# v of one chunk moves from SyncE's queue to a casting DMA on GpSimd's queue

## The chip, the cores and the metric

The kernel runs on one core of a Trainium2 chip. Its metric is the device time of one execution in microseconds (us), the median over several executions. A profile is one further execution, recorded by the hardware profiler; its times are counted from the first instruction of the program.

## What is computed

Two layers in sequence. The first is a retention layer over q, k, v of shape (4 batches, 8 heads, 768 positions, 64):

```
state = gamma[h] * state + outer(k[t], v[t])        # one 64x64 state per batch and head
y[t]  = scale * q[t] @ state
```

The second is an MLP on the 3072 x 512 result: `out = gelu_tanh(y @ w_in) @ w_out`, with w_in 512 x 2048 and w_out 2048 x 512. All inputs and the output are float32 in device memory; the kernel's matmuls take float16.

## The kernel before

**Chunks.** The 768 positions are cut into six chunks c = 0..5 of 128 positions. Inside a chunk, retention becomes matmuls for each of the four batches b: a score matrix a = k q^T (`mm_A`, L273) masked by the decay (`ev_A` on VectorE, L286), y from the old state (`mm_yc`, L295) plus y from the scores and v (`mm_yi`, L308), and the new state from k and v (`mm_s`, L327; evicted by `ev_S`, L344; decayed on GpSimd by `decay`, L353). y, transposed, is the xT of the MLP: `moe1` (L434) with a gelu on ScalarE (L449), then `moe2` (L479), evicted by L501 or L499 and written out by L506.

**Preparation.** q and k come in twice from chunk 2 on. `load_blk` (L110) brings q and k in 32 x 32 blocks, 16 DMAs of 64 KB for each, so that VectorE's 32 x 32 transpose (`tr`, L263) finishes the transposition without TensorE; `load1` (L98) brings v and the plain k with one DMA of 256 KB for each batch. GpSimd multiplies the decay factors into q, kT and k (`prep_blk` L206, `prep1` L195) and casts v to float16 (L192), each into float16 tiles. `prep(c, "QKvk")` is that order: q blocks, kT blocks, v, plain k.

**What sets the order.** The schedule is written out by hand. Every engine executes its instructions in the order in which the program issues them, and waits at the head when an operand is missing. `run(units, after)` (L520) issues a list of matmul units, and after the unit with a given number the extra steps named in the dictionary. So TensorE works on the MLP of chunk c while the retention of chunk c+1 is slipped in between. The stretch of interest is the two `run` calls of chunk 1: the first (L673) does `moe1` of chunk 1, and after its units 7, 8 and 10 prepares chunk 2; the second (L690) does `moe2` of chunk 1 with the retention of chunk 2 in it: after unit 3 come the scores of batches 0 and 1, after 7 those of batches 2 and 3, after 11 `att_Y`, after 12 to 15 the states. The loop at L705 repeats that for the later chunks.

**Queues.** SyncE's queue (SP) holds nearly all loads, one long sequence: q blocks 2, kT blocks 2, three late stores of chunk 0, v 2 (four DMAs), k 2 (four), then `load(3)` = q blocks 3, kT blocks 3 and v and k of chunk 3 in turn, then chunk 4 and so on. GpSimd's queue (POOL) carries, in one order with GpSimd's arithmetic, the weights at the start (w_in L418, w_out L425: float32 in memory, float16 in SBUF, so these DMAs cast) and most stores of the output (L506). Eight semaphores are taken in turn by SP's DMAs, so that each DMA waits for the landing of the eighth before it.

**Buffers.** The raw v tiles have 6 buffers (`v32`), the float16 v tiles 8 (`v16`, two chunks), the raw kT block has one (`kT32`), the raw q block two.

Of the kernel before, what the change touches and what calls it, by code (L numbers as in the profile page):

```python
# [9 lines left out]
F16 = mybir.dt.float16  # L10
# [6 lines left out]
def kernel(  # L17
# [9 lines left out]
    nc = tc.nc  # L27
    B, H, S, Dh = q.shape
    C = 128
# [27 lines left out]
    pre = ctx.enter_context(tc.tile_pool(name="pre", bufs=2 * B))  # L57
# [31 lines left out]
    def ld_tile(nm, c, b):  # L89
        if nm == "q":  # L90
            t = ld_all(("q32", c)).rearrange("p (b hp) a d -> p b (hp a d)", b=B)
            return t[:, b].rearrange("p (h d) -> p h d", h=H)
        if (nm, c, b) not in raw:
            raw[nm, c, b] = ld.tile([128, H, Dh], F32, tag=f"{nm}32", bufs=6, name=f"{nm}32")
        return raw[nm, c, b]

    def load1(eng, nm, c, b):
        eng.dma_start(  # L98
            out=ld_tile(nm, c, b),
            in_=srcs[nm][b, :, c * C:(c + 1) * C, :].rearrange("h p d -> p h d"),  # L100
        )

    def load_blk(nm, c):
        t = ld_all((nm + ("32" if nm == "q" else "T32"), c))
        src = srcs[nm].rearrange("b (hp j) s (dd d) -> j dd s (b hp) d", j=2, dd=2)
        for j in range(2):
            for dd in range(2):
                for a in range(4):
                    p0, t0 = (2 * j + dd) * 32, c * C + a * 32
                    nc.sync.dma_start(  # L110
                        out=t[p0:p0 + 32, :, a, :], in_=src[j, dd, t0:t0 + 32]
                    )

    def load(c):
        for nm in "qk":
            if c in BLK[nm]:
                load_blk(nm, c)
        for b in range(B):
            for nm in "vk":
                load1(nc.sync, nm, c, b)  # L120
# [22 lines left out]
    for j in range(2):  # L143
# [3 lines left out]
        out=iden,  # L147
        in_=iden,
# [7 lines left out]
        out=mask.rearrange("p j hp t -> p (j hp) t"),  # L156
        in_=mask.rearrange("p j hp t -> p (j hp) t"),
# [7 lines left out]
        out=misc[:, 0:1], in_=zero[:, 0:1], func=AF.Gelu_apprx_tanh, scale=1.0  # L165
# [14 lines left out]
    h16 = {}  # L180
# [345 lines left out]
    VE, AC, PO, SY = nc.vector, nc.scalar, nc.gpsimd, nc.sync  # L526
# [132 lines left out]
    load_blk("k", 2)  # L659
    for rows, o_sb in late:  # L660
        nc.sync.dma_start(out=rows, in_=o_sb)
    for nm in "vk":
        for b in range(B):
            load1(SY, nm, 2, b)
    load(3)

    def prep(c, nms):

        for nm in nms:
# [12 lines left out]
            3: [(att_S, 1, 2)],  # L682
            4: [(att_AY, 1, (3,), "o", 1, (), VE)],
            6: [(att_S, 1, 3)],
            7: [(prep, 2, "Q")],
            8: [(tr, 2, "q")],
            10: [(prep, 2, "Kvk")],
        },
    )
    run(  # L690
# [33 lines left out]
    c = NCk - 1  # L724
# [36 lines left out]
```

## Time and profile before

| | us |
|---|---|
| median of 5 executions (lowest to highest) | 213.19 (211.78 to 215.31) |
| the profiled execution's own time | 213.38 |
| its span, first to last instruction | 211.3 |
| TensorE busy in the span | 204.1 (97%) |
| VectorE, ScalarE, GpSimd busy | 91.6, 83.7, 101.1 |
| granted TensorE clock, mean over the span | 1.000 |

The span is 2.1 us shorter than the profiled execution's own time; what lies around it is taken as fixed. The other views used below are the list of waits (who waited for whom: total, times, longest), the timeline (start and length of a group of instructions, in brackets the idle time before it and what ended it) and sums by window (busy time by engine and the mean share of the 16 DMA engines that was busy; it exceeds 1 where packets overlap).

### The profile page before, as it was taken

Reading aid. Unit: us, or ns where it says so; the run is one execution under the profiler, and the core shown is the slowest. Engines: PE = TensorE matmul, PEld = TensorE weight load, DVE = VectorE, ACT = ScalarE, POOL = GpSimd, SP = SyncE. Lnnn points to the kernel's source line nnn. Section 1 sums busy time; section 2 is a strip of 40 time slices with the busy share of each in tenths; the row PEclk is TensorE's granted clock in tenths of the full one; section 3 lists DMA queues with packets and bytes.
Section 4 is the critical chain, followed back from the end, with each engine's and each line's share of the span. In section 5 each row is a group of like instructions: output and inputs, shape, how many; then the busy total and the mean of one; then the engine's idle time right before and its main releaser. Section 6 shows DMA issues by size and latency. Waiting matters only on the chain.

```text
span 211.3 us, 3863 instructions
## 1 busy us (share of the span) xinstructions
PE 204.1 (97%) x1502; PEld 110.3 (52%) x1502; DVE 91.6 (43%) x163; ACT 83.7 (40%) x142; POOL 101.1 (48%) x123
## 2 busy tenths in 40 slices
PE   7999999999999999999699999999999999999994
PEld 2458444467886465444356444456444446444453
DVE  6787000488543848150856542566560562100001
ACT  2474660345464121664113366113366113466120
POOL 2599300316175749571976949561497711100100
PEclk9999999999999999999999999999999999999999
DMA  7999999997878987968988989888898020100112
GB/s 162 288 236 180 206 201 204 278 251 147 125 112 212 244 179 186 204 107 160 254 160 192 210 151 247 158 168 176 168 232 200 3 101 36 67 0 0 50 50 99
DMA packets 132691, 33.83 MB, mean 160 GB/s; under 512 B 126529, under 2 KB 130881, under 8 KB 132673
## 3 DMA queue, kind: packets, MB, share of 16 engines
q1 hardware_dynamic: 115248, 21.27, 52.1%
q0 software_dynamic: 5696, 8.91, 18.0%
q10 hardware_dynamic: 11728, 3.41, 7.1%
q8 instruction: 11, 0.18, 0.3%
q14 instruction: 8, 0.06, 0.1%
HBM read 31.48 MB, written 6.29 MB: 179 GB/s over the span
## 4 chain that ended last, share of the span: by engine, by line
PE 62%; DMA 19%; SPq 10%; POOL 4%; issue 1%; DVE 1%; POOLq 0%; DVEq 0%
PE o_ps L479 29%; PE h_ps L434 26%; SPq L110 9%; DMA w_out<-in_moe_w_out_dram 8%; DMA k<-in_k_dram 7%; DMA q<-in_q_dram 3%; PE a_ps L273 2%; PE y_ps L308 2%; POOL w_in L418 2%; PE y_ps L295 1%; DMA kT<-in_k_dram 1%; PE s_ps L327 1%; POOL k L195 1%; POOL kT L206 1%; DVE a_sb L286 1%
## 5 line engine op out<-in xcount | busy, mean ns | idle before, releaser
L479 PE MATMUL o_ps<-w_out,g 128*128 128x512 f16 (+1 forms) x400 | 88.6, 371 | 0.0
L434 PE MATMUL h_ps<-xT,w_in 128*128 128x512 f16 (+1 forms) x464 | 85.1, 343 | 0.0
L449 ACT ACTIVATE g<-h_ps 128x512 f16<-128x512 f32 x96 | 56.9, 597 | 47.4 <-PE h_ps L434 47.3
L434 PEld LDWEIGHTS <-w_in 128*128 128x128 f16 x464 | 44.9, 98 | 37.5 <-issue 0.3
L479 PEld LDWEIGHTS <-g 128*128 128x128 f16 x400 | 37.4, 98 | 38.6
L286 DVE TENSOR_TENSOR a_sb<-a_ps,mask 128x512 f16<-128x512 f32 x48 | 30.1, 684 | 16.3 <-PE a_ps L273 16.2
L501 ACT COPY o_sb<-o_ps 128x512 f32<-128x512 f32 x19 | 11.1, 585 | 53.0 <-PE o_ps L479 51.2
L195 POOL TENSOR_TENSOR k<-k,cst 128x512 f16<-128x512 f32 x23 | 24.1, 1066 | 15.3 <-DMA k<-in_k_dram 15.2
L506 POOL DMA_DIRECT2D out_dram<-o_sb x18 | 10.0, 559 | 40.3 <-ACT o_sb L501 33.4
L206 POOL TENSOR_TENSOR kT<-kT,cst 128x512 f16<-128x512 f32 x16 | 16.3, 1047 | 11.0 <-DMA kT<-in_k_dram 10.5
L353 POOL TENSOR_TENSOR stg<-st,cst 128x512 f32<-128x512 f16 x16 | 16.4, 1059 | 6.4 <-DVE st L344 3.9
L263 DVE STREAM_TRANSPOSE qkT<-q 128x512 f16<-128x512 f16 x16 | 11.4, 711 | 15.7 <-POOL q L206 15.7
L206 POOL TENSOR_TENSOR q<-q,cst 128x512 f16<-128x512 f32 x16 | 16.3, 1047 | 2.9 <-DMA kT<-in_k_dram 2.8
L263 DVE STREAM_TRANSPOSE qkT<-kT 128x512 f16<-128x512 f16 x16 | 10.9, 698 | 13.5 <-POOL kT L206 13.5
L344 DVE TENSOR_TENSOR st<-s_ps,stg 64x256 f16<-64x256 f32 x32 | 13.5, 422 | 5.0 <-PE s_ps L327 4.4
L195 DVE TENSOR_TENSOR q<-q,cst 128x512 f16<-128x512 f32 x8 | 5.9, 743 | 17.6 <-DMA q<-in_q_dram 17.6
L192 POOL CAST v<-v 128x512 f16<-128x512 f32 x16 | 9.5, 613 | 7.0 <-DMA v<-in_v_dram 4.1
L226 DVE CAST xT<-y_ps 128x512 f16<-128x512 f32 x11 | 7.2, 687 | 12.9 <-PE y_ps L308 12.9
L517 DVE COPY o_sb<-o_ps 128x256 f32<-128x256 f32 x2 | 0.8, 424 | 26.6 <-PE o_ps L479 26.6
L224 ACT CAST xT<-y_ps 128x512 f16<-128x512 f32 x13 | 7.2, 587 | 11.2 <-PE y_ps L308 11.2
L171 PE MATMUL spin_ps<-zero 128*128 128x512 f16 x30 | 9.2, 443 | 1.3 <-DVE zero L139 1.3
L273 PE MATMUL a_ps<-qkT 64*128 64x128 f16 x192 | 8.3, 218 | 1.9 <-DVE qkT L263 1.6
(39 smaller groups left out, 88.5 us busy)
## 6 DMA issues: line engine op xcount, KB each, us to landing
v<-in_v_dram SPq DMA_DIRECT2D x21, 256.0 KB, 4.3
k<-in_k_dram SPq DMA_DIRECT2D x20, 256.0 KB, 4.3
out_dram<-o_sb POOLq DMA_DIRECT2D x18, 256.0 KB, 3.0
q<-in_q_dram SPq DMA_DIRECT2D x64, 64.0 KB, 2.8
kT<-in_k_dram SPq DMA_DIRECT2D x64, 64.0 KB, 2.8
w_out<-in_moe_w_out_dram POOLq DMA_DIRECT2D x4, 512.0 KB, 15.8
q<-in_q_dram ACTq DMA_DIRECT2D x4, 256.0 KB, 8.6
k<-in_k_dram ACTq DMA_DIRECT2D x4, 256.0 KB, 8.4
```

The source lines that it names most:

```text
L110: nc.sync.dma_start(out=t[p0:p0 + 32, :, a, :], in_=src[j, dd, t0:t0 + 32])
L195: eng.tensor_tensor(out=t, in0=src, in1=cst[:, col:col + H].unsqueeze(2).broadcast_to([128, H, Dh]), op=ALU.mult,)
L206: nc.gpsimd.tensor_tensor(out=t, in0=ld_all((key, c))[:, b * NHP:(b + 1) * NHP].rearrange("p hp a d -> p (hp a) d"), in1=cst[:, col:col + ...
L263: nc.vector.transpose(out=qkT_tile(c, b)[:, "qk".index(nm)].rearrange("p hp t -> p (hp t)"), in_=blk16.pop((nm, c, b)).rearrange("p ha d - ...
L273: nc.tensor.matmul(out=ps[j][:, hp], lhsT=t[j * 64:(j + 1) * 64, 1, hp], rhs=t[j * 64:(j + 1) * 64, 0, hp], start=True, stop=True,)
L286: nc.vector.tensor_tensor(out=s, in0=ps[j], in1=mask[:, j], op=ALU.mult)
L344: eng.tensor_tensor(out=st[sl, :, b, sl], in0=s_ps[sl, :, sl], in1=stg[sl, :, b, sl], op=ALU.add,)
L353: nc.gpsimd.tensor_tensor(out=stg[:, :, b], in0=st[:, :, b], in1=cst[:, OG:OG + NHP].unsqueeze(2).broadcast_to([128, NHP, 128]), op=ALU.mult,)
L434: nc.tensor.matmul(out=out, lhsT=w_in_of(fc, kc), rhs=xT[c][:, kc, t0:t1], start=(kc == 0 and first), stop=(kc == NHP - 1), skip_group_che ...
L449: nc.scalar.activation(out=out, in_=in_, func=AF.Gelu_apprx_tanh, scale=1.0)
L479: nc.tensor.matmul(out=ps[:, n0:n1], lhsT=g_sb[c, fc // 2][:, fc % 2, b * C:(b + 1) * C], rhs=w_out_sb[fc // (NF // NO)][:, fc % (NF // NO ...
L501: nc.scalar.copy(out=o_sb, in_=ps)
```

## The change

v of chunk 2 no longer goes through SP, a float32 tile and a cast on GpSimd. Four DMAs on GpSimd's queue read float32 v and write float16 tiles directly. They stand behind the four q preparations of chunk 2 (after unit 7) and so ahead of the kT preparations (after unit 10). GpSimd's four v casts of chunk 2 are gone. SP goes from the late stores straight to k of chunk 2 and on to `load(3)`. Nothing else differs in order on any engine: TensorE, VectorE and ScalarE have the same instructions in the same sequence. All other chunks load v as before.

```diff
     for rows, o_sb in late:
         nc.sync.dma_start(out=rows, in_=o_sb)
-    for nm in "vk":
-        for b in range(B):
-            load1(SY, nm, 2, b)
-    load(3)
+    for b in range(B):
+        load1(SY, "k", 2, b)
+    load(3)
+
+    def load_v16(c):
+
+        for b in range(B):
+            t = pre.tile([128, H, Dh], F16, tag="v16", bufs=2 * B, name="v16")
+            nc.gpsimd.dma_start(
+                out=t, in_=v[b, :, c * C:(c + 1) * C, :].rearrange("h p d -> p h d")
+            )
+            h16["v", c, b] = t
...
-            7: [(prep, 2, "Q")],
+            7: [(prep, 2, "Q"), (load_v16, 2)],
             8: [(tr, 2, "q")],
-            10: [(prep, 2, "Kvk")],
+            10: [(prep, 2, "Kk")],
```

## The prediction

> **What bounds the kernel now.** I read the page first: TensorE is busy for 204.1 of 211.3 us at a granted clock of 1.000, so only its idle time can be won. The list of waits then says for what it idles inside the run, and TensorE's timeline where.
>
> ```profile
> engine line waited for: us in total, times, longest us
> PE a_ps L273 <- DVE qkT L263: 1.6, 2, 1.0
> PE spin_ps L171 <- DVE zero L139: 1.3, 1, 1.3
> ```
> ```profile
> 97.73 2.75 PE L479 MATMUL o_ps<-w_out,g 128*128 128x512 f16 x12
> 101.47 0.40 PE L273 MATMUL a_ps<-qkT 64*128 64x128 f16 x8 [0.99 <-DVE qkT L263]
> 102.48 0.40 PE L273 MATMUL a_ps<-qkT 64*128 64x128 f16 x8 [0.61 <-DVE qkT L263]
> ```
>
> The spin wait is the start-up; the change does not reach it. The only wait of over 0.5 us after it is 0.99 + 0.61 = 1.60 us at 101.5: the scores of chunk 3 wait for the kT transposes of chunk 3. **So the change can win at most 1.6 us, 0.75%.** The other chunks' scores (69.42, 134.11, 165.96) wait for nothing.
>
> Back from there, in the timelines of GpSimd and of SP:
>
> ```profile
> 60.23 4.07 POOL L206 TENSOR_TENSOR q<-q,cst 128x512 f16<-128x512 f32 x4
> 66.72 4.07 POOL L206 TENSOR_TENSOR kT<-kT,cst 128x512 f16<-128x512 f32 x4 [2.43 <-DMA kT<-in_k_dram]
> ...
> 99.62 4.06 POOL L206 TENSOR_TENSOR kT<-kT,cst 128x512 f16<-128x512 f32 x4 [5.20 <-DMA kT<-in_k_dram]
> ```
> ```profile
> 64.86 1.42 SPq L661 DMA_DIRECT2D out_dram<-o_sb  x3
> 66.37 4.42 SPq L98 DMA_DIRECT2D v<-in_v_dram  x4
> 70.84 3.78 SPq L98 DMA_DIRECT2D k<-in_k_dram  x4
> 74.71 13.13 SPq L110 DMA_DIRECT2D q<-in_q_dram  x16
> 87.95 9.30 SPq L110 DMA_DIRECT2D kT<-in_k_dram  x16
> ```
>
> GpSimd stood idle for 5.20 us before the kT preparation of chunk 3, for a DMA that SP issued at the end of an unbroken queue (64.86 to 97.25). SP's order makes the wait: v, k, q, kT. Every microsecond that SP is earlier arrives at 99.62.
>
> **Gain: the stall at 101.5.** Taking v out removes 4.42 us of issue ahead of k. The gain g in the landing of kT lies between 0.5 and 4.4 us. 4.4 is that whole row. For the low end, DMA engines, not SP, set the pace there; the sums by window are:
>
> ```profile
> 64.00:66.00 2.00, 2.00 (x20) 1.77 (x19) 0.75 (x2) 1.24 (x3) 0.30 (x1) 1.00 0.73 115
> 66.00:72.00 6.00, 6.00 (x43) 2.78 (x41) 3.57 (x6) 1.18 (x2) 4.71 (x6) 1.00 1.08 279
> 72.00:77.00 5.00, 5.00 (x38) 2.34 (x37) 4.03 (x7) 0.58 (x1) 2.94 (x5) 1.00 1.06 240
> 77.00:80.00 3.00, 3.00 (x55) 2.21 (x53) 0.71 (x2) 1.59 (x3) 1.67 (x2) 1.00 0.45 76
> ```
>
> The last two columns are the DMA share and GB/s. From 66 to 77 the engines are full (1.06 to 1.08), and v's bytes are still read in the same stretch. If only the idle shares can be filled, that is 2 x 0.27 = 0.5 us at 64 to 66 (low end) and 3 x 0.55 = 1.7 us more at 77 to 80, where SP issues slowly because the k loads before it have not landed. I take the sum of the bytes: SP alone moves 266 GB/s in such 256 KB loads (the DMA view of 99.5 to 104). Stores of 0.79 MB at 330 GB/s (my estimate, between the 426 and 221 of the slices 67 to 69) take 2.4 us, v and k of 2.1 MB take 7.9 us; from about 65.8 that ends at 76.1, with a microsecond to land 77 against 79.9 before: g = 2.9.
>
> As a row and a rule that speak against the change: the engines' share of 1.06 to 1.08 is the row. The Trainium skill, page "DMA: Bandwidth & Descriptors", section "Rules for kernel authors", says the same of queues in general, that spreading DMAs over SP, ACT and GpSimd gives no bandwidth, since all run on the same 16 engines, and saves only issue time. By that rule alone g would be the 0.5 of the first idle stretch, and the time 212.9; no row decides it.
>
> **Cost: the kT preparation of chunk 2.** The four new DMAs are issued by GpSimd between its q preparations, which end at 60.23 + 4.07 = 64.30, and its kT preparations, which start at 66.72 because their DMA lands then. So 2.4 us of issue are covered by an idle gap. What the trace has for an issue by GpSimd:
>
> ```profile
> L506 POOL DMA_DIRECT2D out_dram<-o_sb x18 | 10.0, 559 | 40.3 <-ACT o_sb L501 33.4 <-DMA kT<-in_k_dram 3.9 <-DVE o_sb L499 3.0
> L418 POOL DMA_DIRECT2D w_in<-in_moe_w_in_dram x6 | 4.6, 782 | 0.0
> L425 POOL DMA_DIRECT2D w_out<-in_moe_w_out_dram x4 | 3.0, 801 | 0.0
> ```
>
> A store takes 0.56. The casting loads are 0.72 to 0.91 each, and 0.73 apart when they follow one another (12.38 to 19.05 for nine, the last at full length). They land in pieces of 1 KB, 256 or 512 for one DMA; the 512 cost hardly more than the 256 (0.74 against 0.71 apart). The new DMAs have 1024 pieces each (128 partitions x 8 heads, 256 B read, 128 B written), which no row shows. Bounds: 0.56 (pieces cost nothing) and 2 x 0.73 = 1.46 (all of the cost is by pieces). By the step from 256 to 512, 1024 pieces come to 0.785; this is the nearest row, and I take it. Four end at 64.30 + 3.14 = 67.44, so the kT preparation is late by d = 0.7.
>
> Who waits: the VectorE transposes of kT for batches 0 and 1 end at 68.51 and 69.52 (rows 67.80 and 68.81, 0.71 each); TensorE's scores start at 69.42, the second eight at 69.75. With 0.06 for the signal the second transpose has 0.17 us in hand. So a stall **s = d - 0.17 = 0.55 us** appears at 69.5 where there was none. Batches 2 and 3 have four microseconds more and hide it. Stores late on SP are not touched: ScalarE reuses the first of their buffers at 69.57, against a landing at 67.3 now.
>
> **The rest.** The four casts of v on GpSimd go (4 x 0.61 = 2.44 us); nothing on the path waited for them: the plain k preparations end at 81.28, TensorE wants the last k at 83.69. They now end earlier, with nothing to gain. v itself: TensorE reads it from 78.54 (batch 0) to 79.3 (batch 3), and the cast v was there at 74.5. Now it is the landing that counts. I put its first packets 1.5 us after the first issue, at 65.8 (an estimate: a store of GpSimd's, of 256 KB too, has landed a median 3.0 us after its issue). The nearest row is SP's 256 B packet, 18 ns on one of 16 engines; the weights' 98 ns for a 1 KB piece is the far end. At 18 to 21 ns, taken by turns with SP's (from 29 to 35 us GpSimd's and ACT's packets are moved 948 to 886), v ends near 76 and has landed by 77.1: two microseconds of cover. If the cover goes, each microsecond of lateness beyond 79.3 + s stalls TensorE one for one.
>
> **Sum.** TensorE's scores of chunk 3 would start at 100.48 if nothing were late; they stand still for 1.6 us. Against that time the end moves to max(s, 1.6 - g). With s = 0.55 and g = 2.9 it is 0.55: the old stall is gone, a third of it comes back in front. Net -1.05 us, 213.38 - 1.05 = **212.3 us** for the profiled execution. This execution is 0.2 above the median of the runs shown (213.19), so against the median it is a gain of 0.4 to 0.5%. 0.5%, 1.07 us, is about what a measurement of this kernel can tell from no change.
>
> **The rivals.**
> - *Issues as cheap as a store's* (0.56 each, d = 0): s = 0, all 1.6 us are won, 211.8. For it: 256 and 512 pieces cost the same. Against: the casting loads' own rows. Chance 0.10.
> - *The main case*, 0.71 to 0.94 each (0.94: the slope from a store's 64 pieces to 512, carried on): net -1.3 to -0.4, 212.0 to 212.9. Chance 0.45, the faster half a little likelier (0.28 to 0.17).
> - *SP gains little* (g under 1.1, DMA engines bound): net max(s, 1.6 - g) - 1.6, with g = 0.5 it is -0.5, 212.9. For it: shares over 1 from 66 to 77. Against: 0.45 at 77 to 80. Chance 0.13.
> - *The issue takes the place of the stall.* Four issues of 1024 pieces hold the kT preparation and with it the scores at 69.5. From 1.05 us an issue, s = 4 x 1.05 - 2.42 - 0.17 = 1.6 and nothing is won; at 1.46, s = 3.25, net +1.65, 215.0: slower. Chance 0.17, half of it above +0.5%.
> - *v lands late* (a small casting packet costs over 30 ns): from there a stall at 78.5 of 1 to several us, at 98 ns some 13. A stall of 1.05 us eats the gain; from 2.1 us on it is slower than before by over 0.5%, 214.5 and more. Chance 0.10.
> - Something unseen on GpSimd's queue, slower: 0.05.
>
> **How the numbers follow.** Faster by over 0.5%: 0.28 + 0.10 = 0.38. Within 0.5%: 0.17 + 0.13 + 0.08 = 0.38. Slower: 0.09 + 0.10 + 0.05 = 0.24. The range goes from 211.5 (all won, less the 0.2 that the profiled execution lies above the median) to 215.0 (the dear issue); beyond it lie most of the late v and the unseen, under 0.2.
>
> **What the new profile would show.** Right: no wait of TensorE's scores at about 101, kT of chunk 3 prepared from about 96.7, a new wait of half a microsecond for qkT near 69.5, four issues near 0.8 us between 64.3 and 67.5, v landed by 77. Wrong: issues of over 1 us; a TensorE wait at 78.5 for a DMA of v; kT of chunk 3 landing after 98.

## The result and the profile after

The changed kernel takes a median of 213.49 us (212.36 to 218.22, 48 executions), the kernel before 212.64 us (211.38 to 215.35, 90 executions). The ratio is 1.004, with a 95% interval of 1.0026 to 1.0054 (intervals stand in brackets below): the change costs some 0.85 us, where 0.4 to 0.5% of gain was forecast. The profiled execution of the changed kernel took 213.94 us, span 211.8 us, at a granted clock of 1.00 in every stage shown. One later profile, that of e9_k_on_pool, fell in an execution of 305.14 us at a granted clock of 0.661 and is not read; all others ran at 0.992 to 1.000.

TensorE's list of waits in the changed kernel (total, times, longest):

```profile
PE a_ps L273 <- DVE qkT L263: 1.9, 2, 1.3
PE spin_ps L171 <- DVE zero L139: 1.3, 1, 1.3
```

Its line for qkT read 1.6, 2, 1.0 before. It looks like the same wait, but TensorE's timeline (changed kernel, the two stretches that matter) shows that it is another:

```profile
65.77 3.62 PE L479 MATMUL o_ps<-w_out,g 128*128 128x512 f16 x16
70.65 0.40 PE L273 MATMUL a_ps<-qkT 64*128 64x128 f16 x8 [1.26 <-DVE qkT L263]
71.67 0.40 PE L273 MATMUL a_ps<-qkT 64*128 64x128 f16 x8 [0.61 <-DVE qkT L263]
...
99.74 2.75 PE L479 MATMUL o_ps<-w_out,g 128*128 128x512 f16 x12
102.43 0.62 PE L273 MATMUL a_ps<-qkT 64*128 64x128 f16 x16
```

The wait at 101 is gone (no bracket at 102.43), and a larger one stands at 69.4 to 71.7: the scores of chunk 2 wait 1.26 + 0.61 = 1.87 us for kT of chunk 2, where nothing waited before. GpSimd's timeline (changed kernel) shows what stands in front of that kT:

```profile
60.13 4.07 POOL L206 TENSOR_TENSOR q<-q,cst 128x512 f16<-128x512 f32 x4
64.14 3.57 POOL L670 DMA_DIRECT2D v<-in_v_dram  x4
68.81 4.06 POOL L206 TENSOR_TENSOR kT<-kT,cst 128x512 f16<-128x512 f32 x4 [1.10 <-DMA kT<-in_k_dram]
...
98.13 4.07 POOL L206 TENSOR_TENSOR kT<-kT,cst 128x512 f16<-128x512 f32 x4 [4.92 <-DMA kT<-in_k_dram]
```

Two things delay the kT preparation of chunk 2 from 66.72 to 68.81. The four issues end at 64.14 + 3.57 = 67.71. And then GpSimd still waits 1.10 us for the kT block itself, which landed at 66.66 before and lands at 68.73 now. The landing ends last in this execution. The view of SP's kT issues says that the last of them landed 4.07 us after its issue, the one before it 2.4; before, these were 2.38 and 2.6.

The sums by window (changed kernel; DMA share and GB/s are last) answer to the rows of 66 to 77 shown before:

```profile
66.00:72.00 6.00, 4.12 (x33) 1.82 (x31) 1.78 (x3) 1.16 (x2) 4.90 (x6) 1.00 1.45 210
72.00:77.00 5.00, 5.00 (x41) 2.35 (x38) 4.35 (x8) 0.58 (x1) 2.14 (x3) 1.00 1.54 218
```

The share of the DMA engines is higher (1.45 and 1.54, before 1.08 and 1.06), the bytes per second are lower (210 and 218, before 279 and 240). The second is a matter of counting: the DMA view has each v DMA of GpSimd's with the 128 KB of float16 that it writes, SP's with 256 KB. From 66 to 77 it lists 1.82 MB on SP's queue and 0.52 on GpSimd's; with v's 1.05 MB as read that is 2.87 MB, and before it was 2.87 as well. So no bytes are gained in this stretch: beside v, SP's queue moves the same 1.82 MB as before. SP's timeline (changed kernel) shows its loads held:

```profile
66.74 8.35 SPq L98 DMA_DIRECT2D k<-in_k_dram  x4
75.18 11.78 SPq L110 DMA_DIRECT2D q<-in_q_dram  x16
```

The four k issues take 8.35 us instead of 3.78, about as much as v's 4.42 and k's 3.78 together took before, since the k loads now land 6.2 to 9.4 us after their issue (before 3.9 to 6.3). SP comes to q of chunk 3 at 75.18, against 74.71 before: by then the head start is gone.

The end of the program, from TensorE's timeline (its first line has the span):

```profile
core 0 of [0], span 211.8 us
...
194.41 14.02 PE L479 MATMUL o_ps<-w_out,g 128*128 128x512 f16 x80
```

TensorE ends at 208.43, 0.18 later than before (208.25). From there to the end of the span it is 3.37 us, before 3.09. So this pair of executions nearly adds up: +1.87 at 69.5, -1.60 at 101, +0.28 behind the last matmul = +0.55. The span grew by 0.46 and the time by 213.94 - 213.38 = 0.56; about a tenth of a microsecond is not placed.

### The profile page after: what moved, and what is told of

It reads as the page before. It is cut to its first block, busy times and chain, and to the rows that moved or that the text cites. A ratio compares the mean times of both kernels' runs of the same rounds, so it can differ in the third digit from the quotient of the medians.

```text
span 211.8 us, 3857 instructions
## 1 busy us (share of the span) xinstructions
PE 205.0 (97%) x1502; PEld 110.6 (52%) x1502; DVE 91.8 (43%) x163; ACT 83.5 (39%) x142; POOL 102.1 (48%) x123
## 4 chain that ended last, share of the span: by engine, by line
PE 84%; SPq 8%; DMA 2%; DVE 1%; POOL 1%; issue 1%; ACT 0%
PE o_ps L479 37%; PE h_ps L434 33%; SPq L110 8%; PE spin_ps L171 4%; PE a_ps L273 3%; PE y_ps L308 2%; DMA kT<-in_k_dram 2%; PE y_ps L295 2%; PE s_ps L327 2%; POOL kT L206 1%; PE qkT_ps L239 1%; PE qkT_ps L252 1%; ACT qkT L224 0%; DVE qkT L263 0%; DVE qkT L226 0%
## 5 line engine op out<-in xcount | busy, mean ns | idle before, releaser
L449 ACT ACTIVATE g<-h_ps 128x512 f16<-128x512 f32 x96 | 56.9, 597 | 47.0 <-PE h_ps L434 46.9
L171 PE MATMUL spin_ps<-zero 128*128 128x512 f16 x30 | 10.3, 485 | 1.3 <-DVE zero L139 1.3
L192 POOL CAST v<-v 128x512 f16<-128x512 f32 x12 | 7.1, 609 | 5.8 <-DMA v<-in_v_dram 5.8
```

The lines of the kernel that those rows point to most:

```text
L171: nc.tensor.matmul(out=ps, lhsT=zero[:, 0:128], rhs=zero, start=True, stop=True)
L449: nc.scalar.activation(out=out, in_=in_, func=AF.Gelu_apprx_tanh, scale=1.0)
```

## The experiments

My theory after this result: the change trades the wait at 101 for one at 69.5 that has two causes, the issue time on GpSimd and a later landing of kT beside v's packets; and something at the end costs 0.28. Rivals: the issue time alone is the cause, and the late kT was chance; it is the cast in the DMA; or the wait at 101 is worth less than one profile showed. Diffs are against the changed kernel unless "before" is said. Each ratio is to the kernel before on the same chip.

### The gain by itself: e1_no_v

v of chunk 2 is neither loaded nor cast; chunk 2 takes chunk 1's v. All that the change takes from SP stays taken, and nothing is added on GpSimd.

```diff
-            t = pre.tile([128, H, Dh], F16, tag="v16", ...)
-            nc.gpsimd.dma_start(out=t, in_=v[b, ...])
-            h16["v", c, b] = t
+            h16["v", c, b] = h16["v", c - 1, b]
```

> v of chunk 2 is neither loaded nor cast (chunk 2 takes chunk 1's v): SP's shorter queue without any cost. Theory (the head start pays, and two costs at 69.5 eat it: the issue time on GpSimd and a kT landing delayed by v's packets): no TensorE wait at 69.5, none at 101, 1.6 us under the kernel before (ratio 0.9925). Rival (the old stall at 101 is not set by SP's queue): the wait at 101 stays, no difference to the kernel before.

Measured: 212.19 us, 0.9984 [0.9961, 1.0006]. From TensorE's and GpSimd's timelines:

```profile
68.99 0.40 PE L273 MATMUL a_ps<-qkT 64*128 64x128 f16 x8
69.67 0.40 PE L273 MATMUL a_ps<-qkT 64*128 64x128 f16 x8 [0.28 <-DVE qkT L263]
```
```profile
93.71 4.07 POOL L206 TENSOR_TENSOR kT<-kT,cst 128x512 f16<-128x512 f32 x4 [2.93 <-DMA kT<-in_k_dram]
```

kT of chunk 3 is there at 93.71 instead of 99.62 and nobody waits at 101. Yet the time is only some 0.3 us better. I had expected the full 1.6 us: a miss. Two small losses are in this 0.3: the wait of 0.28 at 69.67, and an end stretch of 3.38 us instead of 3.09, since SP has four DMAs fewer here too (the section on the end). Without them the head start would be worth some 0.9 us (an estimate: 0.3 + 0.3 + 0.3), well under 1.6.

### What the old wait is in another execution: e8_before_again

The kernel before, unchanged, profiled once more.

> The kernel before, unchanged, for a second profile. Theory: the wait at 101.5, 1.6 us in the first profile, varies with the landing of kT of chunk 3 from one execution to the next, and is under 1.2 us here if the execution is near the median. Rival: 1.6 us in each execution.

Measured: 212.54 us, span 210.5. TensorE's timeline:

```profile
101.60 0.40 PE L273 MATMUL a_ps<-qkT 64*128 64x128 f16 x8 [0.61 <-DVE qkT L263]
```

Here the wait at 101 is 0.61, not 1.60: kT of chunk 3 landed 0.9 us earlier. The profile that I predicted from had a span of 211.3, while the median of 212.64 less the 2.1 us around the span is 210.5. It was an unfavourable execution, and its large wait was the very thing to be won. By the medians that wait is worth some 0.8 us (1.6 less 211.3 - 210.5; an estimate). e13_before_4loads, below, is a third profile of this order up to 190 us, and has 0.17 + 0.61 = 0.78 at 101.

### The issue time by itself: e2_issue_only, e5_issue_only

Again chunk 2 takes chunk 1's v; in place of the four large DMAs GpSimd issues five, or seven, casting DMAs of 128 pieces.

```diff
+            h16["v", c, b] = h16["v", c - 1, b]
+        for h in range(5):          # 7 in e5_issue_only
+            t = pre.tile([128, Dh], F16, tag="small", bufs=5, name="small")
+            nc.gpsimd.dma_start(out=t, in_=v[0, h, c * C:(c + 1) * C, :])
```

> Five casting DMAs of GpSimd with 128 pieces each stand where the four with 1024 stood (chunk 2 takes chunk 1's v): the same 3.6 us of issue, an eighth and a bit of the traffic. Theory of two costs: kT of chunk 2 lands at 66.7 as in the kernel before, GpSimd starts on it at 67.7 when its issues end, TensorE waits about 0.9 us at 69.5; ratio 0.9965. Rival (issue time alone makes the stall): the wait at 69.5 is 1.9 us as in the changed kernel, ratio 1.001. Second rival (traffic alone): no wait at 69.5, ratio 0.9925.

Measured: 212.34 us, 0.9999 [0.9973, 1.0024]. The five issues took 2.71 us, 0.54 each, so they were not the 3.6 us that I meant to make; kT landed at 67.11 and its preparation started at 67.18. As a test of the issue time it says nothing, and seven were needed:

> Seven casting DMAs with 128 pieces each in the place of the four with 1024 (chunk 2 takes chunk 1's v): the run with five issued for 2.71 us, 0.54 each, so seven issue for 3.8 us, as long as the changed kernel's 3.57, with a fifth of its packets. Theory of two costs: kT of chunk 2 lands at 66.7 to 67.2, GpSimd starts on it when the issues end, near 67.6, TensorE waits 0.8 to 1.1 us at 69.5; span near 210.7. Rival (issue alone): the wait is 1.9 us, span 211.5. Rival (traffic alone): wait 0.3 us as without v, span 209.8.

Measured: 213.30 us, 1.0026 [0.9997, 1.0054]. GpSimd's and TensorE's timelines:

```profile
64.33 3.77 POOL L672 DMA_DIRECT2D small<-in_v_dram  x7
68.06 4.12 POOL L206 TENSOR_TENSOR kT<-kT,cst 128x512 f16<-128x512 f32 x4
```
```profile
69.98 0.40 PE L273 MATMUL a_ps<-qkT 64*128 64x128 f16 x8 [0.40 <-DVE qkT L263]
70.98 0.40 PE L273 MATMUL a_ps<-qkT 64*128 64x128 f16 x8 [0.61 <-DVE qkT L263]
```

The kT row has no bracket: GpSimd went from the issues straight to kT, which had landed at 67.12. So 3.77 us of issue alone make a stall of 0.40 + 0.61 = 1.01 us, not the 1.87 of the changed kernel. The rest needs v's bytes: in e2_issue_only the first small DMA was 0.63 us ahead of the last kT DMA, which still landed after 2.73.

### The late landing, or chance: e11_after_again

The changed kernel, profiled once more.

> The changed kernel, unchanged, for a second profile. Theory: kT of chunk 2 lands at 68 to 69.2 again, the wait at 69.5 is 1.2 to 2.4 us, none at 101. Rival (the first profile was a chance): kT lands at 66.7 to 67.2 and the wait is about 1 us, that of the issues.

Measured: 213.05 us, span 211.0. GpSimd's and TensorE's timelines:

```profile
64.40 3.57 POOL L670 DMA_DIRECT2D v<-in_v_dram  x4
67.95 4.09 POOL L206 TENSOR_TENSOR kT<-kT,cst 128x512 f16<-128x512 f32 x4
```
```profile
69.84 0.40 PE L273 MATMUL a_ps<-qkT 64*128 64x128 f16 x8 [0.20 <-DVE qkT L263]
70.85 0.40 PE L273 MATMUL a_ps<-qkT 64*128 64x128 f16 x8 [0.61 <-DVE qkT L263]
```

Now kT landed on time (66.51) and the stall is 0.81, the issue time alone. So the late kT of the first profile does not come every time, and the rival was right in this. It is not without a cause, though, as the next kernels show: it goes with which queue is ahead.

### Moving v's DMAs: e6_early, e3_v_after_kT

e6_early issues them first of all after unit 4, in idle time of GpSimd; e3_v_after_kT behind the kT preparations.

```diff
-            7: [(prep, 2, "Q"), (load_v16, 2)],
+            7: [(prep, 2, "Q")],
# e6_early
-            4: [(att_AY, 1, (3,), "o", 1, (), VE)],
+            4: [(load_v16, 2), (att_AY, 1, (3,), "o", 1, (), VE)],
# e3_v_after_kT
-            10: [(prep, 2, "Kk")],
+            10: [(prep, 2, "K"), (load_v16, 2), (prep, 2, "k")],
```

> The four DMAs are triggered after unit 4 of the run, near 56.7 us, in GpSimd's idle time ahead of the q preparations, so their issue delays nothing. Theory of two costs: the packets now run among the kT blocks of chunk 2, kT lands 1.5 to 3 us later than 66.7, TensorE waits 1.3 to 3 us at 69.5; ratio 1.002 to 1.008. Rival (issue alone): kT lands at 66.7 and the wait is gone; ratio 0.996 to 0.998.

Measured: 215.86 us, 1.0112 [1.0073, 1.0150]. GpSimd's and TensorE's timelines:

```profile
56.80 3.57 POOL L670 DMA_DIRECT2D v<-in_v_dram  x4
...
69.92 4.07 POOL L206 TENSOR_TENSOR kT<-kT,cst 128x512 f16<-128x512 f32 x4 [4.47 <-DMA kT<-in_k_dram]
```
```profile
71.77 0.40 PE L273 MATMUL a_ps<-qkT 64*128 64x128 f16 x8 [2.19 <-DVE qkT L263]
72.77 0.60 PE L273 MATMUL a_ps<-qkT 64*128 64x128 f16 x8 [0.61 <-DVE qkT L263]
```

Here the issues cost nothing that anyone waits for: GpSimd stands idle for 4.47 us before kT. v's packets alone do it: kT DMAs that SP issued from 60.4 to 65 took 6.3 falling to 2.8 us to land, SP was held at its semaphores, and its last kT DMA was issued at 67.31 and landed at 69.85. The worst version of all, although v is early and its issue is free.

> The four DMAs are triggered behind the four kT preparations instead of ahead of them. Theory of two costs: no wait at 69.5, kT of chunk 2 lands at 66.7; issues from 70.8 to 74.3, the last v lands near 81 and TensorE waits up to 2 us at 78.5 for it; kT of chunk 3 lands near 97.5; ratio 0.995 to 1.003. Rival (late kT landing comes from SP's own order): the wait at 69.5 stays.

Measured: 213.68 us, 1.0046 [1.0022, 1.0070]. kT of chunk 2 landed at 66.92 and the stall at 69.5 fell to 0.12. TensorE's timeline has the price:

```profile
80.12 0.41 PE L308 MATMUL y_ps<-a_sb,v 128*64 128x128 f16 x8 [0.74 <-DMA v<-in_v_dram]
81.60 0.41 PE L308 MATMUL y_ps<-a_sb,v 128*64 128x128 f16 x8 [1.06 <-DMA v<-in_v_dram]
```

v, issued from 71.0, landed up to 81.55, and y waits 1.80 us for it. v behind kT is too late by two microseconds, v ahead of kT holds kT: for this v there is no good place between.

### Is it the cast: e7_plain

The same place and the same four DMAs, but float32 to float32, with the casts on GpSimd as before.

```diff
-            t = pre.tile([128, H, Dh], F16, tag="v16", ...)
-            nc.gpsimd.dma_start(out=t, in_=v[b, ...])
+            raw["v", c, b] = ld.tile([128, H, Dh], F32, tag="v32p", bufs=B, name="v32")
+            load1(PO, "v", c, b)
...
-            10: [(prep, 2, "Kk")],
+            10: [(prep, 2, "Kvk")],
```

> The four DMAs stand where the change has them, but move float32 to float32; GpSimd casts behind the kT preparations as in the kernel before. Theory (the casting packet of 32 ns, not only the count of packets, fills the engines): packets of 18 ns, kT of chunk 2 lands up to 1 us earlier than the changed kernel's 68.7, the wait at 69.5 is 0.9 to 1.5 us. Rival (any v traffic on a second queue delays kT the same): 1.9 us. Issue time 0.88 each as with the cast, if pieces set it.

Measured: 213.82 us, 1.0055 [1.0027, 1.0083]. GpSimd's timeline:

```profile
63.85 3.57 POOL L98 DMA_DIRECT2D v<-in_v_dram  x4
69.17 4.06 POOL L206 TENSOR_TENSOR kT<-kT,cst 128x512 f16<-128x512 f32 x4 [1.76 <-DMA kT<-in_k_dram]
```

The issue takes the same 3.57 us, and kT lands at 69.10, as late as ever. I had held the small casting packets to be the cause: that part of the theory falls. The four loads of v on GpSimd's queue do it with the cast or without.

### Fewer issues: e10_one_dma, and e15_one_dma_4loads

v of chunk 2 as one casting DMA of 4096 pieces in place of four of 1024.

```diff
+        t = pre.tile([128, B * H, Dh], F16, tag="v16all", bufs=1, name="v16")
+        nc.gpsimd.dma_start(
+            out=t, in_=v[:, :, c * C:(c + 1) * C, :].rearrange("b h p d -> p (b h) d")
+        )
         for b in range(B):
...
+            h16["v", c, b] = t[:, b * H:(b + 1) * H]
```

> The changed kernel with its four DMAs as one of 4096 pieces, at the same place. By 0.54 us for 128 pieces and 0.88 for 1024 an issue costs 0.49 and 0.39 ns a piece, so one DMA takes 2.1 us and ends at 66.2, inside the gap of GpSimd; the same packets move. Theory (the packets delay kT, and that alone makes the wait): kT of chunk 2 lands at 68.4 to 69.2, the wait at 69.5 stays 1.6 to 2.4 us. Rival (issue time makes the wait): kT preparation starts at 66.8 and the wait is 0.3 us at most, ratio 0.997.

Measured: 212.80 us, 1.0004 [0.9981, 1.0027]. GpSimd's timeline:

```profile
64.09 1.75 POOL L669 DMA_DIRECT2D v<-in_v_dram  x1
66.55 4.07 POOL L206 TENSOR_TENSOR kT<-kT,cst 128x512 f16<-128x512 f32 x4 [0.72 <-DMA kT<-in_k_dram]
```

One issue is 1.75 us instead of 3.57 and ends ahead of the landing of kT (66.48). No stall at 69.5 at all, a wait of 0.40 at 101. My theory had kept a stall of 1.6 to 2.4 here: a miss. In this execution SP's last kT DMA had been issued at 63.94, just ahead of v. The same kernel with the four loads that are described with the next pair shows the other case:

> The changed kernel with one DMA of 4096 pieces for v, and the four loads. Theory: no wait at 69.5 over 0.3 us, 0 to 0.8 us at 101, 3.1 us at the end, so the stall and the end are both gone and what is left is the gain of SP's head start, 0.2 to 0.5 us; ratio 0.9975 to 0.9995. Rival (the head start is worth nothing beside v's packets): 1.000 or more.

Measured: 212.74 us, 0.9987 [0.9953, 1.0021]. GpSimd's timeline:

```profile
63.79 1.75 POOL L669 DMA_DIRECT2D v<-in_v_dram  x1
68.01 4.07 POOL L206 TENSOR_TENSOR kT<-kT,cst 128x512 f16<-128x512 f32 x4 [2.48 <-DMA kT<-in_k_dram]
```

v was issued at 63.79, ahead of the last kT DMA (64.75). kT landed at 67.94, and the stall is 0.82 + 0.61 = 1.43, with the issue long over (I had expected none over 0.3: a miss). Side by side, from the DMA issues and landings of each trace:

| execution | first v issue | last kT issue | it lands after | stall at 69.5 |
|---|---|---|---|---|
| changed kernel, first profile | 64.14 | 64.66 | 4.07 | 1.87 |
| e7_plain | 63.85 | 64.58 | 4.52 | 2.54 |
| e15_one_dma_4loads | 63.79 | 64.75 | 3.19 | 1.43 |
| e10_one_dma | 64.09 | 63.94 | 2.54 | 0 |
| e11_after_again | 64.40 | 64.08 | 2.43 | 0.81 |
| e14_after_4loads | 64.39 | 64.30 | 2.61 | 0.80 |

Where v is ahead by half a microsecond or more, the last kT block is 0.6 to 2 us late; where it is not, kT lands in its usual 2.4 to 2.6. The two queues meet within a few tenths, so the same kernel falls on either side from one execution to the next.

### The end of the program: e13_before_4loads, e14_after_4loads

Four tiny SP loads into tiles that nobody reads are added ahead of the last chunk's `moe1`, to the kernel before and to the changed one. They turn the round of SP's eight semaphores by four, which the change had turned by four the other way.

```diff
+    for i in range(4):
+        scr = const.tile([128, 64], F32, name=f"scr{i}")
+        nc.sync.dma_start(out=scr[:, :OKT + 16], in_=cst_h.ap())
     c = NCk - 1
```

> The kernel before with four more loads on SP (26 KB each, into tiles that nothing reads), in its idle time behind the loads of chunk 5, so that the last store takes the DMA semaphore that it has in the changed kernel. Theory: TensorE loses nothing, but from its last matmul to the end of the span it takes 3.4 us instead of 3.1, as in the changed kernel; ratio 1.0013. Rival (the end is longer for another reason, such as GpSimd's DMAs): 3.1 us, ratio 1.000.

Measured: 213.39 us, 1.0022 [0.9995, 1.0049].

```profile
core 0 of [0], span 211.5 us
...
194.13 14.02 PE L479 MATMUL o_ps<-w_out,g 128*128 128x512 f16 x80
```

> The changed kernel with the same four loads, which brings the last store back to the semaphore of the kernel before. Theory: 3.1 us from the last matmul to the end; the wait at 69.5 is 0.8 to 1.9 us as before; ratio to the kernel before 1.0025 instead of 1.004. Rival: 3.4 us, 1.004.

Measured: 213.16 us, 1.0028 [0.9992, 1.0063].

```profile
core 0 of [0], span 210.7 us
...
193.58 14.02 PE L479 MATMUL o_ps<-w_out,g 128*128 128x512 f16 x80
```

In both fences TensorE's last row and the span give the end stretch. For the kernel before plus four loads it is 211.5 - 208.15 = 3.35 (3.09 without them); for the changed kernel plus four it is 210.7 - 207.60 = 3.1 (3.37 without). The other traces agree: all six executions with SP's 179 DMAs of the kernel before end in 3.07 to 3.11 us, and of the eleven with four fewer or four more, ten end in 3.35 to 3.42 (the other is e12_k_on_pool_late, below). So the 0.28 us follows the number of SP's DMAs and nothing else in the change. SP closes the program by waiting for its eight semaphores in a fixed order. With four DMAs fewer, the last store (L518) has an earlier place in that order, and four more waits of some 0.06 us follow its landing.

e13 also shows that the old order is not free of a wait at 69.5: TensorE waits 0.58 us at 70.4 there, besides the 0.78 at 101. With it there are three profiles of each order, and the waits at these two places sum to 1.60, 0.61 and 1.36 before and 1.87, 0.81 and 0.80 after the change. Three are too few to carry a difference of half a microsecond.

### Other ways to the same gain: e4_late_stores, e9_k_on_pool, e12_k_on_pool_late, e16_k_on_pool_4loads

e4_late_stores is the kernel before with its three late stores moved behind `load(3)` (they need three more output buffers). This gives SP the head start without a DMA on GpSimd.

```diff
-    for rows, o_sb in late:
-        nc.sync.dma_start(out=rows, in_=o_sb)
     for nm in "vk":
...
     load(3)
+    for rows, o_sb in late:
+        nc.sync.dma_start(out=rows, in_=o_sb)
```

> The kernel before, with its three late stores moved on SP from ahead of v of chunk 2 to behind the loads of chunk 3, and three more buffers for them; v stays on SP. Theory: a head start of SP that costs GpSimd nothing pays in full: kT of chunk 3 lands 1.5 to 2.4 us earlier, no wait at 69.5, the wait at 101 goes; ratio 0.9925 to 0.994. Rival (SP's position is not what sets the wait at 101): no difference.

Measured: 212.65 us, 1.0005 [0.9986, 1.0023]. GpSimd's timeline:

```profile
96.34 4.07 POOL L206 TENSOR_TENSOR kT<-kT,cst 128x512 f16<-128x512 f32 x4 [5.10 <-DMA kT<-in_k_dram]
```

kT of chunk 3 comes 3.3 us earlier than before and nobody waits at 101, but a wait of 0.29 is at 70.1. I had expected the full gain: a miss. It has a second reason, which this test brought with it: the `moe1` stretches of chunks 2, 4 and 5 take 14.27 us each instead of 13.98. From TensorE's timeline, one line of the kernel before and two of this one:

```profile
149.46 13.98 PE L434 MATMUL h_ps<-xT,w_in 128*128 128x512 f16 x64
```
```profile
148.40 14.27 PE L434 MATMUL h_ps<-xT,w_in 128*128 128x512 f16 x64
179.65 14.27 PE L434 MATMUL h_ps<-xT,w_in 128*128 128x512 f16 x64
```

Here ScalarE has 24 separate semaphore waits among its gelus (L449), one ahead of every second gelu of these three stretches, and every eighth matmul of the first of them starts 0.04 us later than before. Of all the traces only this one and that of e12_k_on_pool_late have either, and both kernels have the seven buffers and the moved stores. That is 0.87 us that no transfer causes. Without it and the 0.29, the head start would be worth some 1.0 us here (an estimate).

The next three put the plain k of chunk 2 on GpSimd's queue instead of v, behind the kT preparations, in float32. k is wanted some four microseconds later than v, so it can stand where v could not.

```diff
-        load1(SY, "k", 2, b)
+        load1(SY, "v", 2, b)
...
+            raw["k", c, b] = ld.tile([128, H, Dh], F32, tag="k32p", bufs=B, name="k32")
+            load1(PO, "k", c, b)
...
-            7: [(prep, 2, "Q"), (load_v16, 2)],
+            7: [(prep, 2, "Q")],
-            10: [(prep, 2, "Kk")],
+            10: [(prep, 2, "K"), (load_k, 2), (prep, 2, "vk")],
```

> k of chunk 2 in the place of v: v stays on SP with its casts, the four plain loads of k (float32) are issued by GpSimd behind the four kT preparations. k is wanted later than v (80.4 to 83.7 against 78.5 to 79.3). Theory (a second queue's load is free only if it starts after kT of chunk 2 has landed and is wanted late enough): kT lands at 66.7 to 67.2, wait at 69.5 of 0.3 us at most, last k lands near 81, no wait at 80 to 84, kT of chunk 3 lands near 96.5, no wait at 101; span 209.9 to 210.3; ratio 0.9975 to 0.9995. Rival (any load of GpSimd's here costs TensorE about what it gives): ratio 1.001 to 1.005, with a wait at 80 to 84.

Measured: 212.45 us, 0.9983 [0.9957, 1.0008].

> k of chunk 2 on GpSimd behind the kT preparations, and the late stores of SP behind the loads of chunk 3 (three more buffers for them). Theory: no wait over 0.3 us from 60 to 140, span 209.7 to 210.2, ratio 0.997 to 0.9995, no better than with k alone, since kT of chunk 3 is early enough already. Rival: the stores at 66 to 69 delay k or v enough that moving them gives another 0.3 us.

This is e9_k_on_pool with the late stores moved as well. Measured: 213.61 us, 1.0033 [1.0009, 1.0057], slower. TensorE's waits do not tell why (0.4 us for k, 0.2 twice, all before 50 us). Two other things do: the same three `moe1` stretches take 14.27 us as in e4_late_stores (0.87 together), and the end stretch is 3.73 us. Of the 0.64 at the end, 0.28 is that of four DMAs fewer; the rest is a pause of 0.36 between two of SP's closing waits (210.15 to 210.51), whose reason is open.

> k of chunk 2 on GpSimd behind the kT preparations (v stays on SP), and the four loads. Theory: wait of 0.3 us at most at 69.5, none at 80 to 84 and at 101, 3.1 us at the end; ratio 0.996 to 0.998, the best of these kernels. Rival: a wait for k at 80 to 84 or the store's delays eat it, ratio 0.999 or more.

This is e9_k_on_pool with the four loads that restore the end. Measured: 212.22 us, **0.9956 [0.9927, 0.9985]**, the only one of all these kernels whose whole interval lies under 1. GpSimd's timeline and TensorE's whole list of waits over 0.1 us:

```profile
66.32 4.06 POOL L206 TENSOR_TENSOR kT<-kT,cst 128x512 f16<-128x512 f32 x4 [2.27 <-DMA out_dram<-o_sb]
70.32 3.56 POOL L98 DMA_DIRECT2D k<-in_k_dram  x4
73.88 2.27 POOL L192 CAST v<-v 128x512 f16<-128x512 f32 x4
76.12 2.04 POOL L195 TENSOR_TENSOR k<-k,cst 128x512 f16<-128x512 f32 x2
78.94 2.04 POOL L195 TENSOR_TENSOR k<-k,cst 128x512 f16<-128x512 f32 x2 [0.79 <-DMA k<-in_k_dram]
```
```profile
PE spin_ps L171 <- DVE zero L139: 1.3, 1, 1.3
```

The bracket at 66.32 names a store of SP's; the kT block itself had landed at 66.25, and the store only at 66.90. The same 3.56 us of issue stand behind kT, so kT starts at 66.32, and k is ready at 80.98. TensorE waits for nothing after the start-up, neither at 69.5 nor at 101. Span 209.2, 1.3 under e8_before_again. That the four loads, and not chance, part it from e9_k_on_pool (0.9983) is not settled: the intervals overlap.

## Why the prediction was wrong, point by point

- **"The change can win at most 1.6 us"**: right for the profiled execution, where 1.6 went. But it is the size of one execution. A second had 0.61 and a third 0.78, and with v left out altogether the kernel gains some 0.3 us [-0.1, 0.8], or 0.9 without its end stretch and its small wait. e16, with neither, gains 0.9 [0.3, 1.6]. I noted that the execution stood 0.2 above the median of five; against 90 executions it is 0.7 above. Against e8_before_again it is 0.84 above, and its wait is 0.99 longer.
- **The issue, "nearest row 0.785, four end at 67.44, s = 0.55"**: mis-sized. 1024 pieces took 0.89 us each (0.94 the first), the upper part of the range that I gave to the main case. By the issue alone the stall is 0.8 to 1.0 (e11, e14, e5); it is 0.82 by the prediction's own sum with the end of the issues at 67.71.
- **The step that failed: "which start at 66.72 because their DMA lands then".** I took the landing of kT as fixed, and compared the end of the issues with it. In the first profile it moved to 68.73, because v's first DMA was issued ahead of SP's last kT block (64.14 against 64.66). The start of the preparation is the later of the two, so they overlap, but the stall became 1.87 instead of 0.55: 0.27 of the difference is the issue, 1.05 the landing. With the 0.28 at the end this is the whole distance between the forecast of -1.05 and the measured +0.56 in this pair of executions. e6_early shows the landing without the issue, e5_issue_only the issue without the landing. I had counted what the moved DMAs do for SP's later loads, not what they do to its earlier ones.
- **"g = 2.9", a head start of SP's kT of chunk 3**: it landed at 97.97, 97.90 and 98.63 (e14), against 99.24, 98.36 and 99.14 (e13) before, so by the means g was some 0.7. Without v's bytes (e1_no_v) it was 5.7. The row with the shares over 1 had said so. The rule quoted from the Trainium skill ("DMA: Bandwidth & Descriptors", "Rules for kernel authors"), that other queues bring no bandwidth, agrees with these landings, and with the 2.87 MB read from 66 to 77 in both kernels. I set it aside for a sum of bytes, and left out that SP's k loads, which share the engines with v, then land later (6.2 to 9.4 us after their issue) and hold SP back. The small g was still enough to end the wait at 101, since TensorE itself arrives there some 1.9 us later.
- **The end** was not in the sum, in which it moves with TensorE's stalls alone: +0.28 us, shown by e13 and e14.
- **Right**: the wait at 101 goes; the new one is at 69.5 and for qkT; v lands at 76.31 (77 predicted) with no wait for it; the four casts that go bring nothing.
- **The rivals**: the nearest was "the issue takes the place of the stall". Its condition, 1.05 us an issue, was not met; the place was right, and the landing supplied the missing price. *SP gains little* came true beside it: a g of some 0.7 is under its 1.1.

By the medians (an estimate): the lost wait is some -0.8 to -1.0, the stall between 0.80 and 1.87, the end +0.28; that is +0.1 to +1.35, around the measured 0.85. The end is the only steady term of the three. How often an execution falls on which side is open, since only three of this order were profiled, one of them with kT late. So is how kT is held: that v's packets take the shared engines fits all six rows of the table and e6_early. While the late block is under way, from 66.5 to 68.5, the DMA view of the changed kernel has 908 packets of GpSimd's queue and 600 of SP's, so the two run side by side; the order within an engine's queue was not seen.

## What to carry to other kernels

A transfer moved to another queue still meets the old queue on the DMA engines, so ask which earlier, urgent load it will overtake, and place it behind that one: of two candidates, move the load that is needed later. Before a wait is taken as the gain, see it in a second profile, above all when the profiled execution is slower than the median. A change in the number of a queue's DMAs can move the end of the program by tenths of a microsecond, which is the size of what is hunted here. And before a variant is booked as a miss, compare the stretches that it should not touch: e4_late_stores lost 0.87 us there.

## What the runs showed of the hardware

- The time of an issue by GpSimd grows with the pieces, though less than in proportion: 0.54 us for 128, 0.88 for 1024, 1.75 for 4096. At 1024 it is the same with and without a cast. The page "DMA: Bandwidth & Descriptors" of the Trainium skill (section "Anatomy of one DMA — SWDGE (gpsimd) path") says that many descriptors go out before an added cost shows; here it showed by 1024 pieces (0.88 against 0.54).
- Four DMAs on GpSimd's queue can hold a 64 KB transfer of SP's from 2.4 to 4.1 and 4.5 us, with a cast or without.
- The closing waits of SP on its semaphores cost some 0.06 us each, and which of them stands last is set by how many DMAs the queue has had.
- A separate semaphore wait ahead of every second gelu of ScalarE goes with 0.04 us for each eighth matmul of TensorE, 0.29 us in a `moe1` stretch (e4_late_stores, e12_k_on_pool_late).
